# Two attention blocks with their gradients: order of the dV and dK stores, K of the first heads, and when the second block's x and g are transposed

## The chip, the core and the metric

The kernel runs on one core of a Trainium2 chip. The metric is the device time of one execution in microseconds. Five runs of the kernel before gave a median of 1718.41 us (1716.88 to 1725.21). The engines of the core are TensorE (PE in the profile, PEld for its weight loads), VectorE (DVE), ScalarE (ACT), GpSimd (POOL) and SyncE (SP). SP computes nothing here: it issues DMAs. POOL computes and issues DMAs.

## The reference

Two independent attention blocks, A and B, have the same shapes: x is 8 x 96 x 640 (batch, queries, model width), the caches of K and V are 8 x 32 x 512 x 128 (batch, heads, keys, head width), wq is 640 x 4096 and wo 4096 x 640, all bfloat16. The forward pass and then all gradients are wanted, for a given gradient of the joined output:

```python
q = (x @ wq).reshape(B, Sq, H, Dh).transpose(0, 2, 1, 3)
scores = jnp.einsum("bhqd,bhkd->bhqk", q, k_cache) * (Dh ** -0.5)
p = softmax(scores)
o = jnp.einsum("bhqk,bhkd->bhqd", p, v_cache)
out = o.transpose(0, 2, 1, 3).reshape(B, Sq, H * Dh) @ wo
```

The outputs are the joined output of both blocks, and for each block dx, dK, dV, dwq and dwo: eleven arrays. The caches read and the gradients dK and dV written are the bulk of the bytes.

## The kernel before

**Items and ticks.** The kernel is unrolled whole. Each piece of work is a Python closure that is handed to an `Emitter` with a tick and a slot; `run` sorts by tick, slot and order of adding, and calls the closures, which record instructions. One tick is one batch of one head: block A begins at tick 13, a head takes 8 ticks, block B begins 256 ticks later. Within a block, `c0t` is the first tick of a head, and `ct` that of a batch. `OFF` (L45) says how many ticks after `ct` each stage of a batch stands, and `HK` (L46) does so for the work of a whole head:

```python
OFF = dict(ldk=-5, ldv=-3, kt=-3, vt=0, s2=3, s3=3, s4=4, s5=5, s6=6, s7=7, s8=8)
HK = dict(pA=-10, pA2=-9, pB=-3, pC0=[-2, 0], pC1=[-1, 0], pD1=1, pD0=2, qA0=18, qA1=17, ...)
```

So eight or so batches are in flight in a tick, each in another stage. A scheduler then takes the recorded instructions and chooses the order on each engine and all waits, by its own estimate of durations, and may move an instruction away from where it was recorded. What goes through `tc.keep_in_program_order` (`pinned`, L111) stays in the recorded order relative to the others of its engine that are pinned. On POOL these are P_sb (L329), prod (L407), and the loads of wq and wo (L190, L199). The stores of dV and dK (L398) are not among them. On SP only the loads of `setup_ld` (L118) are pinned.

**One batch.** `c_ld` (L266) loads K and V of two batches at a time from SP, 256 KB each. `c_xt` (L275) transposes two batches by a DMA transpose from SP: all V (tile VT), and K of every second pair of batches (tile KT). `k_on_pe` (L548) chooses: for the other pairs `c_s1` (L280) transposes K on PE, four 128 x 128 transposes into kT_ps (L285) for each batch, copied out by DVE as KT_pe (L287). Then:

- S = Q K^T on PE (L298); DVE takes the negative row maximum negm (L300); ACT makes E = exp(S) and its row sums (L310).
- DVE inverts the sums (rinv, L320); POOL scales E to P_sb (L329), one tick before it is used.
- PE transposes P (L365); ACT evacuates (L378); PE forms O (L359), and dV from P and the natural dO (L389); ACT evacuates dV into dV_sb (L392).
- POOL multiplies O by dO (prod, L407); PE sums it (dl_ps, L419) and forms dP with VT (L417); DVE combines both with P to dS_sb (L421).
- PE forms dK from dS and the natural Q (L432), ACT evacuates into dK_sb (L435). PE transposes dS (L346) and forms dQ (L340).

dV_sb and dK_sb hold two batches each and have three tiles each. When the second batch is in, `c_st` (L395) stores the 256 KB from POOL's queue (L398). It is recorded one tick after that batch's dV or dK, at slot 54.3, behind P_sb (53) and prod (54). All PSUM tiles share eight banks.

**One head.** `pA` and `pA2` load wq and wo from POOL's queue. `pB` (L210, L216) transposes them. `pC` (L243) forms Q (which = 0) from xT and dO (which = 1) from gT, each in two pieces of 512 and 256 tokens. `pD` (L258) transposes these into natural order: Qnat_h and dOnat_h, evacuated by DVE. qA, qB, qD form dwo and dwq of finished heads, and `gU` (L512) the sums over groups of up to six heads for the output and for dx.

**x and g of a block.** `pC` needs x and g transposed: 12 tiles of 128 tokens, six of x and six of g. In block A they come from x_nat and g_nat. In block B `setup_ld` loads each tile from SP (160 KB) into one of five tiles named ld_tmp, and `setup_T` transposes it on PE (five transposes into tp_ps, L134) with a copy by DVE into xT or gT. The lines L162 to L171 set their ticks. The order is x 0 to 3, g 0 to 3, x 4 and 5, g 4 and 5. From the sixth on, a load must wait until the transposes of the tile five places earlier have read theirs.

Of the kernel before, what the change touches and what calls it, by code (L numbers as in the profile page):

```python
# [30 lines left out]
SL_LOAD = 0  # L31
# [9 lines left out]
SL_HEAD = 90  # L41
# [12 lines left out]
def build_block(tc, em, tick0, blk, x, kc, vc, wq, wo, g_all, out_all, dx, dk, dv, dwq, dwo, ident, ones, pools, HG=6, first=True, groups=None):  # L54
    nc = tc.nc
# [55 lines left out]
    def pinned(ins):  # L111
        return tc.keep_in_program_order(ins)

    def setup_ld(which_, t):
        def f():
            src_flat = x_flat if which_ == 0 else g_flat
            tmp = stp.tile([128, D], BF16, name="ld_tmp", tag="stage")
            pinned(nc.sync.dma_start(tmp[:], src_flat[t * 128:(t + 1) * 128, :]))  # L118
            S[("tmp", which_, t)] = tmp
        return f  # L120
# [41 lines left out]
                nc.vector.tensor_scalar(dst, src, float(sc), None, op0=ALU.mult)  # L162

    xg = [(0, t) for t in range(min(4, TT))] + [(1, t) for t in range(min(4, TT))] + [(w, t) for w in (0, 1) for t in range(4, TT)]
    xg_tick = [-8, -7, -6, -5, -4, -4, -3, -3, -2, -2, -1, -1]
    for i, (which_, t) in enumerate(xg):
        if first:
            em.add(tick0 + (-8 if which_ == 0 else 3), SL_SETUP, setup_T(which_, t))
        else:
            em.add(tick0 + (-12 if i < 5 else xg_tick[i - 5] - 1), SL_LOAD + (0 if i < 5 else 2), setup_ld(which_, t))  # L170
            em.add(tick0 + xg_tick[i], SL_SETUP, setup_T(which_, t))  # L171
    if first:
        for which_, tk in ((0, -12), (1, -11)):
# [53 lines left out]
    def pC(h, which, si):  # L227
        def f():
            st = HS[(blk, h)]
            (t0, w) = tsplits[si]  # L230
            if which == 0:
                dst = st["QT_h"]
                lhs = lambda c: st["wq_h"][:, c, :]
                rhsT = S["xT"]
                sc = scale
            else:
                dst = st["dOT_h"]
                lhs = lambda c: st["woT_h"][:, c * 128:(c + 1) * 128]
                rhsT = S["gT"]
                sc = None  # L240
            q_ps = bank([128, w], F32, "q_ps")
            for c in range(DC):
                nc.tensor.matmul(q_ps[:], lhs(c), rhsT[:, c, t0:t0 + w], start=(c == 0), stop=(c == DC - 1))  # L243
            evac(EV["pC%d%d" % (which, si)], dst[:, t0:t0 + w], q_ps[:], sc)
        return f
# [149 lines left out]
    def c_st(h, b, which):  # L395
        def f():
            dst = dv if which == "v" else dk
            nc.gpsimd.dma_start(dst[b - 1:b + 1, h].rearrange("b (p c) d -> p b (c d)", c=KC), SB.pop((blk, h, b // 2, which))[:])  # L398
        return f

    def c_s5b(h, b):
# [144 lines left out]
    NTS = len(tsplits)  # L546

    def k_on_pe(h, b):  # L548
        return (b // NB) % 2 == 0

    SX = pools["SX"]
    for g in range(NG):
        h0 = GH0[g]
        for hh in range(groups[g]):
            h = h0 + hh
            c0t = tick0 + h * B
            if not (first and h == 0):
                em.add(c0t + HK["pA"], 54.6, pA(h))
                em.add(c0t + HK["pA2"], 54.6, pA2(h))
            em.add(c0t + HK["pB"], SL_HEAD, pB(h))  # L560
            fh = first and h == 0
            for si in range(NTS):
                em.add(c0t + HK["pC0"][min(si, len(HK["pC0"]) - 1)], SL_HEAD, pC(h, 0, si))
                em.add(c0t + (3 if fh else HK["pC1"][min(si, len(HK["pC1"]) - 1)]), SL_HEAD + (7 if fh else 0), pC(h, 1, si))
            em.add(c0t + (3 if fh else HK["pD1"]), SL_HEAD + (8 if fh else 0), pD(h, 1))
            em.add(c0t + (4 if fh else HK["pD0"]), SL_HEAD, pD(h, 0))
            for b in range(B):
                ct = c0t + b
                if b % NB == 0:
                    em.add(tick0 - 12 if first and h == 0 and b == 0 else ct + OFF["ldk"], SLOTS["LOAD"], c_ld(h, b, "K", 7))  # L570
                    em.add(ct + OFF["ldv"], SLOTS["LOAD"], c_ld(h, b, "V", 5))
                    if not k_on_pe(h, b):
                        em.add(ct + OFF["kt"], SLOTS["LOAD"] + 1, c_xt(h, b, "KT", 2))
                    em.add(ct + OFF["vt"], SLOTS["LOAD"] + 1, c_xt(h, b, "VT", 4))
                if k_on_pe(h, b):
                    em.add(ct + 2, SLOTS["S1"], c_s1(h, b))
                em.add(ct + OFF["s2"], SLOTS["S2A"], c_s2a(h, b))
                em.add(ct + OFF["s2"], SLOTS["S2B"], c_s2b(h, b))
                em.add(ct + OFF["s3"], SLOTS["S3A"], c_s3a(h, b))
                em.add(ct + OFF["s3"], SLOTS["S3B"], c_s3b(h, b))  # L580
                em.add(ct + OFF["s5"], SLOTS["S5B"], c_s5b(h, b))
                if b % 2 == 1:
                    em.add(ct + OFF["s4"] + 1, 54.3, c_st(h, b, "v"))
                    em.add(ct + OFF["s7"] + 1, 54.3, c_st(h, b, "k"))
                em.add(ct + OFF["s4"], SLOTS["S4"], c_s4(h, b))
                for i, o in enumerate(("s8", "s7", "s5", "s4")):
                    SX.setdefault(ct + OFF[o], [None] * 4)[i] = (blk, h, b)
                em.add(ct + OFF["s6"], SLOTS["S6"], c_s6(h, b))
                em.add(ct + OFF["s7"], SLOTS["S7"], c_s7(h, b))
            hk = HK if first or h < H - 1 else dict(HK, qA0=13, qB=[14, 15], qA1=16, qD=[(19, 0, 2), (19, 2, 4), (19, 4, 5)])  # L590
            em.add(c0t + hk["qA0"], SL_HEAD, qA(h, 0))
            for di in range(len(wsplits)):
                em.add(c0t + hk["qB"][di], SL_HEAD + 1, qB(h, di))
            em.add(c0t + hk["qA1"], SL_HEAD, qA(h, 1))
            for (k_, c_lo, c_hi) in hk["qD"]:
                if c_lo < DC and h % 2 == 1:
                    em.add(c0t + k_, SL_HEAD + 2, qD(h, c_lo, min(c_hi, DC)))
        cLg = tick0 + (h0 + groups[g] - 1) * B + B - 1
        gs0 = max(3, (GSPREAD0 * groups[g]) // HG)
        gs1 = max(3, (GSPREAD1 * groups[g]) // HG)  # L600
        if not first and g == NG - 2:
            gs0, gs1 = 9, 9
        if g == 0:
            em.add(cLg + OFF["s5"] - 2, SL_LOAD, setup_acc)
        subs = [(0, t, gi) for t in range(TT) for gi in range(len(gsplits))] + [(1, t, gi) for t in range(TT) for gi in range(len(gsplits))]
        n_out = TT * len(gsplits)
        for i, (which, t, gi) in enumerate(subs):
            if which == 0:
                tk = cLg + OFF["s5"] + 2 + (i * gs0) // n_out
            else:  # L610
                tk = cLg + OFF["s8"] + 2 + gs0 - 3 + ((i - n_out) * gs1) // n_out
            em.add(tk, SL_GRP, gU(g, which, t, gi))
# [124 lines left out]
```

## Time and profile before

| | |
|---|---|
| median of 5 runs | 1718.41 us (1716.88 to 1725.21) |
| the profiled execution, its own time | 1712.33 us |
| its span, first to last instruction | 1710.5 us |
| PE busy | 1680.1 us, 98% |
| ACT, DVE, POOL busy | 81%, 77%, 61% |
| packets of SP's DMA queue, as a share of 16 engines | 73.1% |
| packets of POOL's DMA queue | 31.7% |
| mean granted TensorE clock | 0.996 |
| DMA issues: dV_sb, dK_sb stores | 256 each, 256 KB, 4.9 and 5.2 us to landing |
| DMA transposes VT, KT | 256 and 128, 6.0 and 4.9 us to landing |

A line of the profile names the source line, the engine, the operation, what it writes and reads, then the shapes and the count, busy time and mean duration. Behind the last bar is the time that the engine stood idle just before such instructions, and what ended that. Matmuls are pipelined, so the duration of one is longer than the distance between two starts. In lines of windows each engine's busy time is followed by its number of instructions; then come the granted clock, the share of the DMA engines and GB/s. In the list of waits a line reads: who waited, for what, total us, times, longest.

### The profile page before, as it was taken

To read this page: it belongs to the slowest core of one execution; us is meant where nothing else is said; L and a number is where in the kernel's file an instruction comes from. 1 tells how busy PE (TensorE), PEld (TensorE's weight loads), DVE (VectorE), ACT (ScalarE), POOL (GpSimd) and SP (SyncE) were. 2 spreads that over 40 slices of the span, in tenths; PEclk is the share of its full clock that TensorE was granted. 3 is DMA by queue.
4 is the path that set the end of the run, shared out by engine and by line. 5 is a ranking of instruction groups with operands and counts; after the bars stand their busy time and mean duration, and the time that the engine had idled before them with its cause. 6 is when DMAs were issued, how large, how long until landed. Compare 5 with 4: busy or idle time off the path is not lost.

```text
span 1710.5 us, 57281 instructions
## 1 busy us (share of the span) xinstructions
PE 1680.1 (98%) x21976; PEld 1343.5 (79%) x21976; DVE 1322.1 (77%) x3040; ACT 1384.7 (81%) x3518; POOL 1046.8 (61%) x1747
## 2 busy tenths in 40 slices
PE   8999999999999999999999999999999999999999
PEld 6787788778778778778778777887788778778876
DVE  6886678778788778788778776787788778778777
ACT  7998789768869869869768897997799679868974
POOL 4666566556657647657567564675576557656754
PEclk9999999999999999999999999999999999999999
DMA  9999999999999989999999999999999989999993
GB/s 267 255 269 267 244 227 244 259 241 255 255 223 267 265 219 272 270 208 282 263 254 248 250 274 247 251 240 257 245 255 275 236 221 262 252 239 244 263 236 132
DMA packets 606770, 424.66 MB, mean 248 GB/s; under 512 B 425696, under 2 KB 564320, under 8 KB 606496
## 3 DMA queue, kind: packets, MB, share of 16 engines
q1 hardware_dynamic: 552912, 243.65, 73.1%
q0 software_dynamic: 53584, 177.35, 31.7%
q8 instruction: 172, 2.82, 0.7%
q14 instruction: 102, 0.84, 0.2%
HBM read 161.09 MB, written 159.12 MB: 187 GB/s over the span
## 4 chain that ended last, share of the span: by engine, by line
PE 87%; DMA 5%; ACT 2%; POOL 2%; issue 2%; DVE 1%; SPq 0%; DVEq 0%; POOLq 0%; ACTq 0%
PE o_ps L512 12%; PE q_ps L243 11%; PE S_ps L298 6%; PE dK_ps L432 6%; PE dV_ps L389 6%; PE dwq_ps L490 6%; PE dP_ps L417 6%; PE dwo_ps L470 6%; PE x_ps L365 5%; PE x_ps L340 5%; PE dst_ps L346 5%; PE x_ps L359 4%; PE kT_ps L285 3%; PE n_ps L258 3%; DMA KT<-K_sb 3%; PE nat_ps L455 3%
## 5 line engine op out<-in xcount | busy, mean ns | idle before, releaser
L329 POOL TENSOR_SCALAR P_sb<-E_sb,rinv 96x512 bf16<-96x512 bf16 x512 | 352.2, 688 | 377.5 <-DVE rinv L320 367.8
L310 ACT ACTIVATE E_sb<-S_ps,negm 96x512 bf16<-96x512 f32 x512 | 355.2, 694 | 205.9 <-DVE negm L300 183.3
L421 DVE SCALAR_TENSOR_TENSOR dS_sb<-dP_ps,dl_ps,P_sb 96x512 bf16<-96x512 f32 x512 | 382.9, 748 | 68.9 <-PE dl_ps L419 51.0
L300 DVE TENSOR_REDUCE negm<-S_ps 96x1 f32<-96x512 f32 x512 | 347.5, 679 | 56.1 <-PE S_ps L298 52.9
L435 ACT ACTIVATE dK_sb<-dK_ps 128x512 bf16<-128x512 f32 x512 | 307.1, 600 | 65.8 <-PE dK_ps L432 61.2
L392 ACT ACTIVATE dV_sb<-dV_ps 128x512 bf16<-128x512 f32 x512 | 316.2, 618 | 0.0
L398 POOL DMA_DIRECT2D out_dram<-dV_sb x256 | 193.7, 757 | 135.2 <-ACT dV_sb L392 126.7
L378 ACT ACTIVATE PT_sb<-x_ps 128x384 bf16<-128x384 bf16 x512 | 257.7, 503 | 1.1 <-PE x_ps L365 1.1
L398 POOL DMA_DIRECT2D out_dram<-dK_sb x256 | 192.6, 752 | 84.0 <-ACT dK_sb L435 53.6
L512 PEld LDWEIGHTS <-OD 128*128 128x128 bf16 x1536 | 132.1, 98 | 99.8 <-issue 0.2
L417 PE MATMUL dP_ps<-VT,dOT_h 128*96 128x512 bf16 x512 | 195.7, 382 | 4.0 <-DMA VT<-V_sb 3.0
L389 PE MATMUL dV_ps<-dOnat_h,P_sb 96*128 96x128 bf16 x2048 | 198.4, 219 | 1.0 <-DVE dOnat_h L160 0.8
L432 PE MATMUL dK_ps<-Qnat_h,dS_sb 96*128 96x128 bf16 x2048 | 198.6, 220 | 0.0
L407 POOL TENSOR_TENSOR prod<-OD,dOT_h 128x96 bf16<-128x96 bf16 x512 | 186.1, 364 | 9.1 <-ACT OD L375 5.1
L348 DVE COPY dST_sb<-dst_ps 128x384 bf16<-128x384 bf16 x512 | 177.0, 346 | 11.8 <-PE dst_ps L346 10.8
L365 PE MATMUL x_ps<-ident,P_sb 96*128 96x96 bf16 x2048 | 172.5, 206 | 4.3 <-POOL P_sb L329 3.1
L375 ACT ACTIVATE OD<-x_ps 128x192 bf16<-128x192 f32 (+1 forms) x515 | 172.6, 335 | 4.5 <-PE x_ps L340 3.8
L320 DVE RECIPROCAL rinv<-rowsum 96x1 f32<-96x1 f32 x512 | 79.4, 155 | 124.0 <-ACT E_sb L310 118.1
L346 PE MATMUL dst_ps<-ident,dS_sb 96*128 96x96 bf16 x2048 | 172.6, 206 | 0.5 <-DVE dS_sb L421 0.5
L359 PE MATMUL x_ps<-PT_sb,V_sb 128*128 128x96 bf16 x2048 | 172.6, 206 | 0.4 <-ACT PT_sb L378 0.4
L340 PE MATMUL x_ps<-dST_sb,K_sb 128*128 128x96 bf16 x2048 | 171.2, 206 | 0.4 <-ACT PT_sb L378 0.4
L340 PEld LDWEIGHTS <-K_sb 128*128 128x128 bf16 x2048 | 132.0, 98 | 25.2 <-issue 1.0
(83 smaller groups left out, 3717.4 us busy)
## 6 DMA issues: line engine op xcount, KB each, us to landing
out_dram<-dV_sb POOLq DMA_DIRECT2D x256, 256.0 KB, 4.9
out_dram<-dK_sb POOLq DMA_DIRECT2D x256, 256.0 KB, 5.2
K_sb<-in_A_k_cache_dram SPq DMA_DIRECT2D x128, 256.0 KB, 5.1
V_sb<-in_A_v_cache_dram SPq DMA_DIRECT2D x128, 256.0 KB, 5.1
K_sb<-in_B_k_cache_dram SPq DMA_DIRECT2D x128, 256.0 KB, 4.9
V_sb<-in_B_v_cache_dram SPq DMA_DIRECT2D x128, 256.0 KB, 5.0
out_dram<-dwo_sb POOLq DMA_DIRECT2D x63, 160.0 KB, 4.9
out_dram<-dwq_sb POOLq DMA_DIRECT2D x31, 320.0 KB, 5.6
```

The costliest lines, as they stand in the source:

```text
L300: nc.vector.tensor_reduce(negm[:], S_ps[:], axis=AX.X, op=ALU.max, negate=True)
L310: nc.scalar.activation(E_sb[:], st["S_ps"][:], ACT.Exp, bias=st["negm"][:], scale=1.0, accum_out=rowsum[:])
L329: pinned(nc.gpsimd.tensor_scalar(P_sb[:], st["E_sb"][:], st["rinv"][:], 0.0, op0=ALU.mult, op1=ALU.add))
L340: nc.tensor.matmul(dQT_ps, st["K_sb"][:, c, :], st["dST_sb"][:, c * Sq:(c + 1) * Sq], start=(c == 0), stop=(c == KC - 1))
L389: nc.tensor.matmul(dV_ps[:, c * 128:(c + 1) * 128], P_sb[:, c * 128:(c + 1) * 128], hs["dOnat_h"][:, b * 128:(b + 1) * 128], start=True, s ...
L392: nc.scalar.activation(SB[(blk, h, b // 2, "v")][:, b % 2], dV_ps[:], ACT.Identity, scale=1.0)
L398: nc.gpsimd.dma_start(dst[b - 1:b + 1, h].rearrange("b (p c) d -> p b (c d)", c=KC), SB.pop((blk, h, b // 2, which))[:])
L417: nc.tensor.matmul(dP_ps[:], hs["dOT_h"][:, tok], st["VT"], start=True, stop=True)
L421: nc.vector.scalar_tensor_tensor(dS_sb[:], dP_ps[:], dl_ps[:, 0:1], st["P_sb"][:], op0=ALU.subtract, op1=ALU.mult)
L432: nc.tensor.matmul(dK_ps[:, c * 128:(c + 1) * 128], dS_sb[:, c * 128:(c + 1) * 128], hs["Qnat_h"][:, b * 128:(b + 1) * 128], start=True, s ...
L435: nc.scalar.activation(SB[(blk, h, b // 2, "k")][:, b % 2], dK_ps[:], ACT.Identity, scale=1.0)
L512: nc.tensor.matmul(o_ps[:], src[:, t * 128:(t + 1) * 128], rhs, start=(hh == 0), stop=(hh == groups[g] - 1))
```

## The change

It has three parts.

First, the store in `c_st` is pinned: stores of dV and dK now keep their recorded place on POOL among P_sb, prod and the pinned loads. In the built program the dV store stands one tick further back on POOL than before and the dK store one or two. Stores of dwo, dwq and of the output are still placed by the scheduler, around these.

Second, `k_on_pe` is also true for head 0 of each block. Batches 2, 3, 6 and 7 of these two heads get four PE transposes and a DVE copy each (8 groups, 32 transposes), and four DMA transposes of KT leave SP's queue.

Third, in block B the transposes of x and g stand two to three ticks later, from tick -6 to tick 2 around the block's start in place of -8 to -1. The first five loads are spread over ticks -11 to -7 in place of all standing at -12, and each later one is recorded one tick behind the transposes that free its tile, no longer one tick ahead of them. All stand behind the tick's loads and DMA transposes of K and V. To fit, head 0 of block B gets its own ticks for the second piece of Q (2), both pieces of dO (1 and 3), and both natural orders (3 and 4); those of dO are put behind the x and g transposes of the tick. Head 0 of block A keeps its ticks.

```diff
-    xg_tick = [-8, -7, -6, -5, -4, -4, -3, -3, -2, -2, -1, -1]
+    xg_tick = [-6, -5, -4, -3, -2, -2, -1, -1, 0, 1, 1, 2]
     for i, (which_, t) in enumerate(xg):
         if first:
             em.add(tick0 + (-8 if which_ == 0 else 3), SL_SETUP, setup_T(which_, t))
         else:
-            em.add(tick0 + (-12 if i < 5 else xg_tick[i - 5] - 1), SL_LOAD + (0 if i < 5 else 2), setup_ld(which_, t))
+            em.add(tick0 + (i - 11 if i < 5 else xg_tick[i - 5] + 1), SL_LOAD + 2, setup_ld(which_, t))
             em.add(tick0 + xg_tick[i], SL_SETUP, setup_T(which_, t))
...
-            nc.gpsimd.dma_start(dst[b - 1:b + 1, h].rearrange("b (p c) d -> p b (c d)", c=KC), SB.pop((blk, h, b // 2, which))[:])
+            pinned(nc.gpsimd.dma_start(dst[b - 1:b + 1, h].rearrange("b (p c) d -> p b (c d)", c=KC), SB.pop((blk, h, b // 2, which))[:]))
...
     def k_on_pe(h, b):
-        return (b // NB) % 2 == 0
+        return (b // NB) % 2 == 0 or h == 0
...
+            p0, p1, d1, d0, late = HK["pC0"], HK["pC1"], HK["pD1"], HK["pD0"], 0
+            if fh:
+                p1, d1, d0, late = [3, 3], 3, 4, 7
+            elif h == 0:
+                p0, p1, d1, d0, late = [-2, 2], [1, 3], 3, 4, 7
             for si in range(NTS):
-                em.add(c0t + HK["pC0"][min(si, len(HK["pC0"]) - 1)], SL_HEAD, pC(h, 0, si))
-                em.add(c0t + (3 if fh else HK["pC1"][min(si, len(HK["pC1"]) - 1)]), SL_HEAD + (7 if fh else 0), pC(h, 1, si))
-            em.add(c0t + (3 if fh else HK["pD1"]), SL_HEAD + (8 if fh else 0), pD(h, 1))
-            em.add(c0t + (4 if fh else HK["pD0"]), SL_HEAD, pD(h, 0))
+                em.add(c0t + p0[min(si, 1)], SL_HEAD, pC(h, 0, si))
+                em.add(c0t + p1[min(si, 1)], SL_HEAD + late, pC(h, 1, si))
+            em.add(c0t + d1, SL_HEAD + (8 if late else 0), pD(h, 1))
+            em.add(c0t + d0, SL_HEAD, pD(h, 0))
```

## The prediction

> **What bounds the kernel now.** I first read the page's busy times, then the wait list, then PE's groups, then the places where PE stands still.
>
> ```profile
> span 1710.5 us, 57281 instructions
> PE 1680.1 (98%) x21976; PEld 1343.5 (79%) x21976; DVE 1322.1 (77%) x3040; ACT 1384.7 (81%) x3518; POOL 1046.8 (61%) x1747
> ```
>
> PE is busy for 98% and so the bound. It leaves 1710.5 - 1680.1 = 30.4 us, and only a part of that is in reach: 5.4 us of gaps lie in the first 39 us and some 4 us behind the last matmul, both untouched. A change can win by closing gaps, and loses whatever it adds to PE. The next view is PE by group; the idle time before each group, with its releaser, is at the end of the line.
>
> ```profile
> L417 PE MATMUL dP_ps<-VT,dOT_h 128*96 128x512 bf16 x512 | 195.7, 382 | 4.0 <-DMA VT<-V_sb 3.0 <-DVE dST_sb L348 0.8 <-DVE rinv L320 0.2
> L365 PE MATMUL x_ps<-ident,P_sb 96*128 96x96 bf16 x2048 | 172.5, 206 | 4.3 <-POOL P_sb L329 3.1
> L298 PE MATMUL S_ps<-KT,QT_h 128*96 128x512 bf16 x256 | 98.0, 383 | 6.7 <-DMA KT<-K_sb 6.5
> L134 PE MATMUL tp_ps<-ident,ld_tmp 128*128 128x128 bf16 x60 | 6.5, 223 | 3.1 <-DMA ld_tmp<-in_grad_out_dram 2.9
> ```
>
> Three kinds of gap remain: transposed K or V late from the DMA queue (10.7 us), P late from POOL (4.3), and one wait for a loaded tile of g (3.1). The third is a single hole. PE's order of time and the granted clock (the column after the bracketed counts of POOL) around it:
>
> ```profile
> 830.24 0.44 PE L134 MATMUL tp_ps<-ident,ld_tmp 128*128 128x128 bf16 x5
> 833.62 0.23 PE L134 MATMUL tp_ps<-ident,ld_tmp 128*128 128x128 bf16 x1 [2.94 <-DMA ld_tmp<-in_grad_out_dram]
> ```
> ```profile
> 822.00:830.00 8.00, 7.83 (x103) 6.05 (x102) 7.05 (x18) 6.52 (x17) 5.61 (x9) 1.00 1.17 326
> 830.00:838.00 8.00, 5.06 (x47) 4.10 (x46) 2.90 (x7) 3.74 (x10) 2.94 (x6) 0.79 1.12 271
> 950.00:960.00 10.00, 7.16 (x85) 5.37 (x83) 6.02 (x13) 5.71 (x15) 5.17 (x9) 0.84 1.11 266
> ```
>
> A gap is paid twice: behind it the clock is halved for a while. In 830 to 838 us the mean is 0.79, so 0.21 x 8 = 1.7 us more are lost. The hole around 955 us costs 0.16 x 10 = 1.6 us within that window too.
>
> **The change, part by part.** Work is laid out in ticks, one batch of one head each; 64 heads of 8 batches in 1710.5 us make 3.3 us per tick.
>
> *x and g of the second block.* All 12 loads, 60 transposes and 12 DVE copies stay; they move. The last load left SP late, as the chain of waits shows:
>
> ```profile
> 825.82 7.76 DMA ld_tmp<-in_grad_out_dram
> ```
>
> It was issued at 825.8, wanted at 830.7 and landed at 833.6. A load cannot go before the transposes that free its tile (5 tiles), and here these stood at tick -3, the use at tick -1: two ticks of cover, less the SP queue. Now release and use are at ticks -1 and 2: three ticks, some 10 us against the 7.8 this load took. On SP the five first loads no longer go out in one burst ahead of loads of K and V, but one per tick behind them, and those that had to wait for a tile no longer stand ahead of K, V and VT. I take the whole hole as gone: -2.9 - 1.7 = -4.6 us. Bounds: 0 (another load is late instead) and -4.6.
> [...]
>
> *The other half of that move.* The first head's Q and dO products and their transposes (L243, L258) fall into ticks -2 to 4, with the transposes of dO straight behind their last product. In the first block, which always had this order, PE waited 0.7 us for gT and 0.8 us for dOnat_h. DVE must take four late xT/gT copies (0.49 each) and four more KT_pe copies (0.40) here, 3.6 us. In the rows of 838 to 862 us it is busy 7.43, 6.09 and 5.47 of 8 each, so 5.0 us are free, and the cover is thin. Cost between 0 and 2.5 us; I take 1.0, near the two waits of the first block. What would be late next is negm, then E and P of those ticks.
>
> *K of the first heads.* Batches 2, 3, 6, 7 of two heads: 8 groups of four transposes more, and 4 DMA transposes fewer (of 384). The pace of such a group stands in the chain:
>
> ```profile
> 433.54 0.22 PE kT_ps L285 x4
> ```
>
> 8 x 0.22 = +1.8 us on the bound engine, fully paid. [...] The 219 ns mean of such a matmul here is its own duration and overlaps the next; starts are 55 ns apart, and the clock stays at 1.00. I take 1.8; the end for the range is 8.8. The 8 evacuations (0.40 each) are DVE's, counted above for the second block; in the first DVE is busy 27.1 of 36 us from 10 to 46 us, so they fit. What it saves: S_ps waits for no KT in either first head (first wait at 70.9 us, in head 2), and SP issues 4 x 1.3 us less, with the DMA engines relieved by as many transfers. Direct gain 0. Whether the relief reaches the late KT of heads 2 to 5 is open: the SP queue is tied to PE by its 7 K tiles, so I take 0, and keep the bound below.
>
> *dV and dK stores.* In the built program they now stand behind P_sb and prod of their tick; before, the scheduler pulled the dV store one tick and the dK store one or two ticks ahead, where it waited for ACT:
>
> ```profile
> POOL out_dram L398 <- ACT dV_sb L392: 129.7, 236, 1.9
> POOL out_dram L398 <- ACT dK_sb L435: 55.4, 45, 3.2
> ```
>
> While the store waits, the next P_sb is queued behind it, and PE's transposes of P (L365) behind that. The sharpest case in POOL's order of time:
>
> ```profile
> 1580.30 0.76 POOL L398 DMA_DIRECT2D out_dram<-dV_sb  x1 [0.54 <-ACT dV_sb L392]
> 1582.98 0.72 POOL L398 DMA_DIRECT2D out_dram<-dK_sb  x1 [1.93 <-ACT dV_sb L392]
> 1583.75 0.70 POOL L329 TENSOR_SCALAR P_sb<-E_sb,rinv 96x512 bf16<-96x512 bf16 x1
> ```
>
> PE then stood 1.2 us. Moved back one tick, a store finds its data ready: no store waits for ACT in the new program. What is it worth? Three gaps before L365 (0.9, 0.6, 1.2) make 2.7. But matmul ends are modelled and hide small delays, so I went over starts: the first transpose of P normally starts 0.17 us after the matmul before it, and what exceeds that sums to 10.8 us; the part where P_sb began right behind a store of dK or dwq or a load of wq is 3.5 + 0.3 + 0.9 = 4.7 us. I take -4.5; bounds -2.7 and -10.8. The cost: the staging tiles (3 each) come free later. From issue and landing times, the dV store moves by 3.2 us and the dK store by 3.7 (medians); 3 of 506 would then land after their tile's next write, by 1.1, 0.1 and 0.7 us. ACT has 19% idle, so 0; if it had none, +1.8.
>
> *Sum:* -4.6 + 1.0 + 1.8 - 4.5 = -6.3 us. Against the profiled execution: 1712.33 us (span 1710.5 and 1.8 around it) goes to 1706.0. The median of the runs, 1718.4, lies 6.1 above that execution; I let that stand and take the same 6.3 off: 1712.1 us, 0.37% less. A difference of 0.3%, 5.2 us, is about what a measurement of this kernel tells from no change.
>
> **Rivals.**
> Nothing to measure: the g load is late again at tick 2 (0 in place of -4.6), the rest as above: 1.0 + 1.8 - 4.5 = -1.7, 1716.7 us. For it: three of the g and x loads took over 4.8 us around the hole, and SP is throttled by the same K, V and VT issues. Against: a tick more of cover.
>
> More than forecast: stores that alternate, one per tick, in place of pairs within 1.5 us shorten the transfers of KT and VT. These waits are 10.7 us of gaps, and two of the three clock dips (1.7 us at 134 and 3.4 us at 957) follow them. Half of 15.8 is 7.9: -14.2, 1704.2 us. For it: the lost 6.1 us between profile and median may be more such waits. Against: the packets of the two queues already fill 73.1 + 31.7% of the engines, and the bytes stay.
>
> Slower: the later stores run into their staging tiles. ACT's next dV or dK copy waits for the landing, then the bank of dV_ps or dK_ps, then PE. The place is the lean heads (2 to 5 of a block), where stores took 8 to 10.7 us. At the median landing of 4.9 and 5.2 us three are late. Were all stores 3 us slower, 16 of dV and 24 of dK would be, by 22.5 + 26.1 = 48.6 us together; a quarter passed on to PE is 12.2, and -6.3 + 12.2 = +5.9, 1724.3 us. It decides from a median landing of about 8 us on. Against: the bytes of the stores don't grow.
>
> **How the numbers follow.** Forecast 0.45 (two thirds of its width, about 1709 to 1716 us, below 1713.3, so 0.32 faster and 0.13 same); nothing 0.13; more 0.23; slower 0.19 (0.17 past +0.3%, 0.02 same). Faster 0.55, same 0.28, slower 0.17. Time: 1712.1. The range reaches to the second rival's 1704.2 less 1.2, as the POOL bound of -10.8 allows, and up to 1722, short of the last one's centre, with its upper part, the 8.8 us of transposes among it, left out: 1703 to 1722.
>
> **What would show it.** No wait of tp_ps for ld_tmp and clock 1.00 through that stretch; POOL's waits for dV_sb and dK_sb near zero, that time now standing as P_sb for rinv, and L365's idle below 2 us; 1056 kT_ps matmuls at 0.22 us per four, PE's busy time up by no more than 2 us; KT 124 times. Wrong if a tp_ps or n_ps group shows a new gap over 1 us, if ACT's dV_sb or dK_sb wait for an out_dram landing, or if L298 and L417 wait more than 10.7 us together.

## The result, and the profile after

The changed kernel takes 1713.0 us (median, 1696.9 to 1739.2) against 1718.2 us of the kernel before beside it (1705.5 to 1743.4): a ratio of 0.9959 with a 95% interval of 0.9942 to 0.9976, 0.41% less. The ratio leaves out slow runs, those over 1.5% above the fastest of their own kernel, which here cuts the changed kernel at 1722.4 us and the one before at 1731.1 us and so flatters the change: the means of all runs give 0.9971. The forecast was 1712.1 us. The same kernel was measured twice more, and gave 0.9986 and 1.0016 (below). So the number was met in the first comparison, but a gain of that size does not repeat, and the parts of the sum came out very differently from what I wrote.

The profiled execution of the changed kernel took 1719.92 us, 7 us above the median of its runs, while that of the kernel before lay 6 us below its own. The two pages must be read for their gaps, not for their spans.

The page's head and the groups by line of the changed kernel, the same ones as shown of the kernel before:

```profile
span 1718.1 us, 56912 instructions
PE 1685.4 (98%) x22008; PEld 1348.4 (78%) x22008; DVE 1324.3 (77%) x3048; ACT 1382.3 (80%) x3518; POOL 1037.6 (60%) x1747
```
```profile
L417 PE MATMUL dP_ps<-VT,dOT_h 128*96 128x512 bf16 x512 | 196.6, 384 | 5.5 <-DMA VT<-V_sb 5.5
L365 PE MATMUL x_ps<-ident,P_sb 96*128 96x96 bf16 x2048 | 172.4, 206 | 1.2 <-POOL P_sb L329 0.8
L298 PE MATMUL S_ps<-KT,QT_h 128*96 128x512 bf16 x248 | 94.2, 380 | 1.2 <-DMA KT<-K_sb 0.6 <-ACT dK_sb L435 0.5
L134 PE MATMUL tp_ps<-ident,ld_tmp 128*128 128x128 bf16 x60 | 6.9, 236 | 9.8 <-DMA ld_tmp<-in_grad_out_dram 8.0 <-DMA ld_tmp<-in_B_x_dram 1.7
```

Read the idle time behind the last bar. The wait for P (L365) fell from 4.3 to 1.2 us. The waits for KT and VT together fell from 10.7 to 6.7 us. The wait for x and g (L134), which was to vanish, rose from 3.1 to 9.8 us. In POOL's list of waits (who waited for what: total us, times, longest) the stores are gone from the top:

```profile
POOL P_sb L329 <- DVE rinv L320: 585.2, 423, 12.8
POOL out_dram L398 <- issue: 12.8, 12, 1.4
...
POOL out_dram L398 <- ACT dK_sb L435: 2.4, 1, 2.4
```

By group, POOL stood idle for 219.2 us before the stores of dV and dK in the kernel before (135.2 and 84.0); now it is 21.0 us (11.8 and 9.2). The time went to P_sb, which waited 367.8 us for rinv before and 585.2 now: POOL is no less idle, but it now stands at P_sb itself, for what P_sb needs.

The hole at the start of the second block, in PE's order of time:

```profile
834.09 0.44 PE L134 MATMUL tp_ps<-ident,ld_tmp 128*128 128x128 bf16 x5
842.57 0.29 PE L134 MATMUL tp_ps<-ident,ld_tmp 128*128 128x128 bf16 x1 [8.04 <-DMA ld_tmp<-in_grad_out_dram]
```

and in the windows of 8 us (busy time of PE, PEld, DVE, ACT, POOL with their counts, then the granted clock, DMA share, GB/s):

```profile
822.00:830.00 8.00, 8.00 (x111) 6.87 (x109) 6.09 (x15) 6.37 (x19) 4.02 (x7) 1.00 1.19 239
830.00:838.00 8.00, 4.24 (x52) 2.95 (x49) 4.06 (x10) 4.36 (x11) 4.40 (x8) 0.95 1.15 281
838.00:846.00 8.00, 3.44 (x34) 3.16 (x35) 1.84 (x5) 1.50 (x4) 0.66 (x1) 0.50 1.14 278
```

PE stood 8.04 us, from 834.53 to 842.57. The clock was 0.50 in the whole window from 838 us, which holds the rest of that gap and 3.4 us behind it. Why the tile of g came late is seen in the order of issue on SP's queue (start, time on the queue):

```profile
825.30 0.72 SPq L266 DMA_DIRECT2D K_sb<-in_A_k_cache_dram  x1
826.08 0.63 SPq L118 DMA_DIRECT2D ld_tmp<-in_grad_out_dram  x1
826.80 2.81 SPq L275 DMA_TRANSPOSE VT<-V_sb  x1
832.38 1.30 SPq L275 DMA_TRANSPOSE KT<-K_sb  x1
833.78 0.67 SPq L266 DMA_DIRECT2D V_sb<-in_A_v_cache_dram  x1
834.54 0.43 SPq L118 DMA_DIRECT2D ld_tmp<-in_grad_out_dram  x1
```

The tile that this last load writes was free at 821.1 us, when the transposes that read it had ended. The load left at 834.5, behind a VT transpose that held the queue for 2.8 us and a KT transpose that waited until its K, issued at 825.3, had landed at 832.3. It landed at 842.5.

### The profile page after: what moved, and what is told of

It reads as the page before. It is cut to its first block, busy times and chain, and to the rows that moved or that the text cites. A ratio compares the mean times of both kernels' runs of the same rounds, so it can differ in the third digit from the quotient of the medians.

```text
span 1718.1 us, 56912 instructions
## 1 busy us (share of the span) xinstructions
PE 1685.4 (98%) x22008; PEld 1348.4 (78%) x22008; DVE 1324.3 (77%) x3048; ACT 1382.3 (80%) x3518; POOL 1037.6 (60%) x1747
## 3 DMA queue, kind: packets, MB, share of 16 engines
q0 software_dynamic: 53584, 177.35, 32.7%
## 4 chain that ended last, share of the span: by engine, by line
PE 89%; DMA 6%; ACT 2%; issue 1%; DVE 1%; POOL 0%; SPq 0%; DVEq 0%; ACTq 0%; POOLq 0%
PE o_ps L512 12%; PE q_ps L243 12%; PE S_ps L298 6%; PE dP_ps L417 6%; PE dV_ps L389 6%; PE dK_ps L432 6%; PE dwo_ps L470 6%; PE dwq_ps L490 5%; PE x_ps L365 5%; PE x_ps L340 5%; PE dst_ps L346 5%; PE x_ps L359 5%; PE kT_ps L285 3%; PE n_ps L258 3%; PE nat_ps L455 3%; DMA VT<-V_sb 1%
## 5 line engine op out<-in xcount | busy, mean ns | idle before, releaser
L329 POOL TENSOR_SCALAR P_sb<-E_sb,rinv 96x512 bf16<-96x512 bf16 x512 | 350.6, 685 | 593.3 <-DVE rinv L320 585.2
L417 PE MATMUL dP_ps<-VT,dOT_h 128*96 128x512 bf16 x512 | 196.6, 384 | 5.5 <-DMA VT<-V_sb 5.5
L398 POOL DMA_DIRECT2D out_dram<-dV_sb x256 | 194.5, 760 | 11.8 <-issue 8.3
L407 POOL TENSOR_TENSOR prod<-OD,dOT_h 128x96 bf16<-128x96 bf16 x512 | 183.2, 358 | 14.7 <-ACT OD L375 13.4
L365 PE MATMUL x_ps<-ident,P_sb 96*128 96x96 bf16 x2048 | 172.4, 206 | 1.2 <-POOL P_sb L329 0.8
L340 PE MATMUL x_ps<-dST_sb,K_sb 128*128 128x96 bf16 x2048 | 171.3, 206 | 0.4 <-ACT PT_sb L378 0.4
L340 PEld LDWEIGHTS <-K_sb 128*128 128x128 bf16 x2048 | 131.9, 98 | 24.9 <-issue 0.8
```

The costliest lines, as they stand in the source:

```text
L329: pinned(nc.gpsimd.tensor_scalar(P_sb[:], st["E_sb"][:], st["rinv"][:], 0.0, op0=ALU.mult, op1=ALU.add))
L340: nc.tensor.matmul(dQT_ps, st["K_sb"][:, c, :], st["dST_sb"][:, c * Sq:(c + 1) * Sq], start=(c == 0), stop=(c == KC - 1))
L398: pinned(nc.gpsimd.dma_start(dst[b - 1:b + 1, h].rearrange("b (p c) d -> p b (c d)", c=KC), SB.pop((blk, h, b // 2, which))[:]))
L417: nc.tensor.matmul(dP_ps[:], hs["dOT_h"][:, tok], st["VT"], start=True, stop=True)
```

## The experiments

Each ratio is to the kernel before, run beside it in the same comparison. The gaps of PE are one profiled execution each: P is the wait of L365; KT + VT those of L298 (for KT) and L417; x/g that of L134 for ld_tmp.

| kernel | median, us | ratio (95% interval) | P | KT + VT | x/g |
|---|---|---|---|---|---|
| before | 1718.2 to 1714.8 | 1 | 4.3 | 10.7 | 3.1 |
| whole change, first | 1713.0 | 0.9959 (0.9942 to 0.9976) | 1.2 | 6.7 | 9.8 |
| whole change, second | 1711.9 | 0.9986 (0.9963 to 1.0010) | 1.2 | 4.5 | 8.6 |
| whole change, third | 1719.2 | 1.0016 (0.9989 to 1.0044) | 1.2 | 6.3 | 4.5 |
| stores only | 1718.4 | 1.0025 (0.9999 to 1.0050) | 1.1 | 11.7 | 6.7 |
| K on PE only | 1711.9 | 1.0002 (0.9980 to 1.0024) | 4.7 | 11.4 | 6.7 |
| x/g move only | 1722.8 | 1.0033 (1.0003 to 1.0063) | 4.3 | 25.6 | 4.8 |
| without the stores | 1716.9 | 1.0011 (0.9983 to 1.0039) | 4.6 | 9.1 | 3.9 |
| without the x/g move | 1712.7 | 0.9984 (0.9959 to 1.0009) | 1.2 | 2.6 | 6.9 |
| the same again | 1716.4 | 1.0003 (0.9978 to 1.0028) | 1.2 | 7.1 | 8.2 |
| x/g loads earlier in the tick | 1715.4 | 1.0005 (0.9971 to 1.0039) | 1.3 | 3.4 | 4.5 |
| K loads 2 ticks earlier | 1763.4 | 1.0274 (1.0216 to 1.0333) | 1.2 | 32.7 | 11.7 |
| more K on PE, no x/g move | 1712.1 | 0.9988 (0.9966 to 1.0011) | 1.2 | 2.3 | 6.2 |
| the same, x/g with cover | 1708.9 | 0.9981 (0.9956 to 1.0006) | 1.2 | 9.9 | 4.3 |

**The whole change, again.** No edit.

> The changed kernel once more, for a second profile and as the measure for its parts. The first profiled execution lost 9.8 us before tp_ps (8.0 of them in one wait for a tile of g at 834 us) and 12 us of clock, and took 1719.9 us against a median of 1713.0. If SP's lag behind its recorded place is a matter of the single execution, this one shows another sum of waits for ld_tmp, anywhere from 0 to 10 us, and the time follows it. If the move of x and g itself makes the wait, it stands here again with 5 us or more. Ratio to the kernel before 0.996 in both cases.

> The changed kernel once more, beside the two below on the same chip. If the whole gains what its two first comparisons had between them, its ratio to the kernel before is 0.996 to 0.999; P waits of L365 near 1.2 us, store waits of POOL near 21 us, S_ps for KT and dP_ps for VT 4 to 7 us together, tp_ps for ld_tmp 7 to 10 us.

Measured 0.9986 and 1.0016. The three intervals of one and the same kernel, 0.9942 to 0.9976 and 0.9989 to 1.0044 among them, do not all overlap: from one comparison to the next the ratio shifts by more than the interval of one comparison says. The means of all runs, 0.9971, 0.9976 and 1.0002, each with some 0.0023 on both sides, lie closer together. The mean of the three ratios is 0.9987. So no difference of 0.2% between two lines of the table is shown by the times; what follows rests on gaps that repeat in every profile. The groups of the second profile (first fence) and the third:

```profile
L365 PE MATMUL x_ps<-ident,P_sb 96*128 96x96 bf16 x2048 | 172.3, 205 | 1.2 <-POOL P_sb L329 0.8
L134 PE MATMUL tp_ps<-ident,ld_tmp 128*128 128x128 bf16 x60 | 6.9, 235 | 8.6 <-DMA ld_tmp<-in_grad_out_dram 8.6
```
```profile
L298 PE MATMUL S_ps<-KT,QT_h 128*96 128x512 bf16 x248 | 94.4, 380 | 6.3 <-DMA KT<-K_sb 5.7 <-ACT dK_sb L435 0.5
L134 PE MATMUL tp_ps<-ident,ld_tmp 128*128 128x128 bf16 x60 | 6.6, 227 | 4.5 <-DMA ld_tmp<-in_grad_out_dram 4.5
```

The gap for x and g is there in both, though in the third it is 4.5 us where I expected 7 to 10, and the third ratio missed its expectation of 0.996 to 0.999. KT is late in the third by as much as in the kernel before (6.3 and 6.7 us).

**The stores alone.** The kernel before with one edit:

```diff
-            nc.gpsimd.dma_start(dst[b - 1:b + 1, h]...)
+            pinned(nc.gpsimd.dma_start(dst[b - 1:b + 1, h]...))
```

> Only the pinned stores of dV and dK. By the prediction's step: POOL's waits for dV_sb and dK_sb fall from 185 us to below 20, the idle time of PE before its transposes of P from 4.3 to below 2 us, and the time by 4.5 us: ratio 0.9974. If the stores also shorten the transfers of KT and VT, PE's idle time before S_ps and dP_ps falls from 10.7 us to half and the ratio to 0.993. If later stores run into their three tiles, ACT waits for landings of out_dram and the ratio is above 1.

```profile
L417 PE MATMUL dP_ps<-VT,dOT_h 128*96 128x512 bf16 x512 | 196.4, 384 | 6.8 <-DMA VT<-V_sb 6.8
L365 PE MATMUL x_ps<-ident,P_sb 96*128 96x96 bf16 x2048 | 172.6, 206 | 1.1 <-POOL P_sb L329 0.6
L298 PE MATMUL S_ps<-KT,QT_h 128*96 128x512 bf16 x256 | 98.3, 384 | 4.9 <-DMA KT<-K_sb 4.9
```

The wait for P goes to 1.1 us, as in every kernel with pinned stores (1.1 to 1.3 us in all ten profiles), against 4.3 to 4.7 us in the four without. KT + VT stay at 11.7 us, as before (10.7): in this profile the stores alone don't shorten those waits. The ratio is 1.0025, and its interval (0.9999 to 1.0050) leaves out the 0.9974 that was expected. ACT waits for no landing of a store in this profile, so late stores are not seen to be the reason. The shorter wait for P is shown, a gain in time from the stores alone is not.

**K of the first heads alone.**

```diff
-        return (b // NB) % 2 == 0
+        return (b // NB) % 2 == 0 or h == 0
```

> Only K of the first heads on PE. By the prediction's step: 32 matmuls kT_ps more at 55 ns, PE's pace otherwise the same: +1.8 us, ratio 1.001. If four DMA transposes fewer relieve the lean heads behind the first ones, the late KT of heads 2 to 5 goes and the ratio is 0.998 or less.

```profile
L417 PE MATMUL dP_ps<-VT,dOT_h 128*96 128x512 bf16 x512 | 196.2, 383 | 10.7 <-DMA VT<-V_sb 10.7
L365 PE MATMUL x_ps<-ident,P_sb 96*128 96x96 bf16 x2048 | 172.5, 206 | 4.7 <-POOL P_sb L329 3.2
L298 PE MATMUL S_ps<-KT,QT_h 128*96 128x512 bf16 x248 | 94.5, 381 | 0.7 <-DMA KT<-K_sb 0.6
```

The wait for KT falls from 6.7 to 0.7 us and that for VT rises from 4.0 to 10.7: the sum stays (11.4). The time stays too, at 1.0002, although 1.8 us of PE work came in.

**The move of x and g alone.** The ticks, the loads and the ticks of head 0, without the other two parts; that is, the changed kernel with two lines taken back:

```diff
-            pinned(nc.gpsimd.dma_start(dst[b - 1:b + 1, h]...))
+            nc.gpsimd.dma_start(dst[b - 1:b + 1, h]...)
...
-        return (b // NB) % 2 == 0 or h == 0
+        return (b // NB) % 2 == 0
```

> Only the move of the second block's x and g, with the ticks of its first head. By the prediction's step: the wait for ld_tmp goes, with its half clock, and 1.0 us is lost behind the products of dO: -3.6 us, ratio 0.998. If the loads are late because they stand behind the loads and transposes of K and V on SP, which lags there, the waits for ld_tmp stay at 3 us or more and the ratio is between 0.999 and 1.002.

1.0033 (1.0003 to 1.0063), not faster and rather slower. PE still waits 4.8 us for a tile, here one of x at 833 us. Its profiled execution was a long one (span 1731.2 us), so its 25.6 us for KT and VT are not held against the move.

**Everything without the stores, and everything without the move.** The changed kernel with `pinned(...)` taken off the stores; and the changed kernel with the ticks, loads and head ticks of the kernel before (the lines of the head ticks are left out here):

```diff
-            pinned(nc.gpsimd.dma_start(dst[b - 1:b + 1, h]...))
+            nc.gpsimd.dma_start(dst[b - 1:b + 1, h]...)
```
```diff
-    xg_tick = [-6, -5, -4, -3, -2, -2, -1, -1, 0, 1, 1, 2]
+    xg_tick = [-8, -7, -6, -5, -4, -4, -3, -3, -2, -2, -1, -1]
...
-            em.add(tick0 + (i - 11 if i < 5 else xg_tick[i - 5] + 1), SL_LOAD + 2, setup_ld(which_, t))
+            em.add(tick0 + (-12 if i < 5 else xg_tick[i - 5] - 1), SL_LOAD + (0 if i < 5 else 2), setup_ld(which_, t))
```

> The change without its first part: K of the first heads on PE and the move of x and g. PE's idle time before its transposes of P is back at 4.3 us. If the stores bring 4.5 us, as the prediction has it, the ratio is above that of the whole change by 0.0026. If it is K on PE together with the move that shortens the waits for KT and VT (6.7 and 4.5 us in the two profiles of the whole, 10.7 before), these stay below 7 us here. If that needs the stores too, they are at 10 us or more.

> The change without its third part: pinned stores and K of the first heads on PE, x and g of the second block as before. In the two profiles of the whole change the waits for ld_tmp were 9.8 and 8.6 us with 5 us of half clock behind them, against 3.1 and 1.7 before. If the move makes them, they are 3 to 6 us here and the ratio is 0.995 or less. If they come with the pinned stores (alone: 6.7) or with K on PE (alone: 6.7), they stay at 6 us or more and the ratio is that of the whole change or above, 0.998 to 1.002.

> Stores and K on PE, without the move of x and g, once more, side by side with the whole. If the move of x and g brings nothing (theory), within 0.002 of the whole in this job. If it was worth the forecast 4.6 us less 1.0, it is 0.002 slower (rival); if the later x and g loads cost what their longer gap in the profile of the changed kernel shows (8.0 against 2.9 us), it is 0.003 faster.

Without the stores the ratio is 1.0011, and the wait for P is back at 4.6 us. That is 0.0024 above the mean of the whole change, near the 0.0026 that the stores were to bring, but its interval (0.9983 to 1.0039) is too wide to show it. KT + VT are 9.1 us there, between the two marks set for them. Without the move it is 0.9984 and, measured again, 1.0003, beside the whole change at 1.0016 in that same comparison. Taking the move out costs nothing that can be seen. The gap for x and g says the same: where x and g stand as in the kernel before, it is 3.1, 6.7, 6.7, 6.9, 8.2 and 6.2 us (mean 6.3); with the move it is 9.8, 8.6, 4.5, 4.8 and 3.9 us (mean 6.3). The 3.1 us of the kernel before, from which I forecast, are the lowest of the six with the old ticks.

**Loads of x and g ahead of the tick's other loads.** The changed kernel with its transposes spread from tick -8 to 2, the first five loads together at tick -14, and all loads ahead of those of K and V in their tick:

```diff
-    xg_tick = [-6, -5, -4, -3, -2, -2, -1, -1, 0, 1, 1, 2]
+    xg_tick = [-8, -7, -6, -5, -4, -3, -2, -1, 0, 1, 2, 2]
...
-            em.add(tick0 + (i - 11 if i < 5 else xg_tick[i - 5] + 1), SL_LOAD + 2, setup_ld(which_, t))
+            em.add(tick0 + (-14 if i < 5 else xg_tick[i - 5] + 1), SL_LOAD - 1, setup_ld(which_, t))
```

> The changed kernel with other ticks for x and g alone: the first five loads together at tick -14, each later one ahead of the tick's loads of K and V one tick behind the release of its tile, the transposes at -8, -7, -6, -5, -4, -3, -2, -1, 0, 1, 2, 2. That gives each load three to ten ticks until its use, in place of two to five. If the waits for ld_tmp are short cover against a lagging SP queue, they fall from 9 us to below 3, the half clock there goes, and the time falls by some 8 us against the whole change: ratio 0.992. If the loads are late whatever their place, since the DMA engines are full there, 6 us or more stay and the ratio is 0.997.

1.0005, with a gap of 4.3 us at 828 us; the 4.5 us in all lie between the two marks set for them (below 3, and 6 or more). The load behind that gap, the seventh, left SP 21.3 us after its tile was free, though it was recorded at the head of its tick. So a place ahead in the tick does not make it early.

**K loads two ticks earlier.** SP's transposes of K wait long for K to land. If that wait were what holds up SP, earlier K loads should help. The changed kernel with eight K tiles (to make room, the matmuls that warm up PE at the start are narrowed from 128 to 96 columns, not shown here):

```diff
-OFF = dict(ldk=-5, ldv=-3, ...)
+OFF = dict(ldk=-7, ldv=-3, ...)
...
-  c_ld(h, b, "K", 7))
+  c_ld(h, b, "K", 8))
```

> The changed kernel with eight tiles of K in place of seven, and the load of K two ticks earlier (the warm-up matmuls are narrowed to 96 columns to make room). SP's queue stands still when a KT transpose waits for its K to land (327 us in all before). If this wait is what makes KT, VT and the loads behind it late, PE's waits for them (KT, VT and ld_tmp: 14 to 16 us in the two profiles of the whole change) fall by half or more, and the ratio is 0.993 or less. If they are late because the DMA engines are full, nothing changes: 0.997.

It is 2.7% slower, which neither expectation had. The wait did go: in SP's list of waits the two lines that stood at 164.5 and 163.0 us in the kernel before are now

```profile
SPq L275 <- DMA K_sb<-in_B_k_cache_dram: 3.9, 2, 3.0
SPq L275 <- DMA K_sb<-in_A_k_cache_dram: 2.9, 1, 2.9
```

but the transfers became longer: medians from issue to landing went from 4.9 to 7.8 us for KT, 6.0 to 7.4 for VT, 5.1 to 6.5 (block A) and 4.9 to 5.8 (block B) for K, and 4.9 to 6.6 for the stores of dV. The times of the two queues' packets add up to 72.9 + 35.5% of the engines' time, beside 73.1 + 31.7% before; that more in flight only makes each wait longer is my reading of this, not shown apart. PE waits for VT and KT 32.7 us, for x and g 11.7:

```profile
L417 PE MATMUL dP_ps<-VT,dOT_h 128*96 128x512 bf16 x512 | 197.5, 386 | 18.4 <-DMA VT<-V_sb 18.3
L298 PE MATMUL S_ps<-KT,QT_h 128*96 128x512 bf16 x248 | 95.0, 383 | 14.3 <-DMA KT<-K_sb 14.1 <-ACT dK_sb L435 0.2
```

SP stood 327 us for K in the kernel before. Issuing K earlier took that wait away and won nothing back.

**More K on PE.** The version without the x/g move, with the K of three heads of each block on PE:

```diff
-        return (b // NB) % 2 == 0 or h == 0
+        return (b // NB) % 2 == 0 or h <= 2
```

> As the one above, but K of heads 0, 1 and 2 of each block is transposed on PE, not only of head 0: 16 more groups at 0.22 us, +3.5 us of PE, and 8 DMA transposes of KT fewer. If each group of heads moved to PE relieves the KT and VT transfers behind it as the first did (10.7 to some 4 us for two heads), the waits of S_ps and dP_ps fall by 2 to 4 us more, and it comes out even with the one above, within 0.001. If the relief was all in the first heads, PE's 3.5 us is paid in full: 0.002 slower.

KT + VT fell to 2.3 us, beside 7.1 and 2.6 of the two profiles of the version it starts from; 3.5 us of PE work came in; the ratio is 0.9988 beside 1.0003. It came out at least even, which speaks against "paid in full" (0.002 slower) and proves no gain.

**Real cover for x and g.** The version above with a sixth ld_tmp tile, transposes from tick -10 on, and loads three to five ticks ahead of their use:

```diff
-    xg_tick = [-8, -7, -6, -5, -4, -4, -3, -3, -2, -2, -1, -1]
+    xg_tick = [-10, -9, -8, -7, -6, -5, -4, -4, -3, -2, -2, -1]
...
-            em.add(tick0 + (-12 if i < 5 else xg_tick[i - 5] - 1), SL_LOAD + (0 if i < 5 else 2), setup_ld(which_, t))
+            em.add(tick0 + (i - 16 if i < 6 else xg_tick[i - 6] + 1), SL_LOAD, setup_ld(which_, t))
...
-            stp=P(name="stp", bufs=5),
+            stp=P(name="stp", bufs=6),
```

> As e11_more_pe (pinned stores, K of heads 0 to 2 on PE), but x and g of the second block get real cover on SP's queue: six tiles ld_tmp in place of five, the first six loads one per tick at ticks -16 to -11, transposes from tick -10 to -1, every later load recorded one tick behind the release of its tile and three to five ticks (10 to 16 us) ahead of its use, at the head of the tick on SP. In all profiles so far the loads 6 to 8 left SP 3.5 to 18 us behind the release of their tile and landed 2.7 to 9.5 us after. If the wait of tp_ps for ld_tmp is a matter of that cover alone (theory), it falls from 6.2 us to under 2, the clock keeps 1.00 around it, and the time is 0.001 to 0.004 below that of e11_more_pe (0.9988): 0.995 to 0.998. If the queue slips by as much again whatever is recorded (rival), tp_ps still waits over 4 us and the ratio stays at 0.998 to 1.001.

0.9981, and the wait is 4.3 us, over the bound of 4 that was set for it: the queue slips again. In SP's order of issue:

```profile
811.96 1.31 SPq L275 DMA_TRANSPOSE VT<-V_sb  x1
816.20 1.27 SPq L275 DMA_TRANSPOSE KT<-K_sb  x1
817.57 1.19 SPq L118 DMA_DIRECT2D ld_tmp<-in_B_x_dram  x1
```

The tile of this load, the tenth, was free at 802.3 us, when the transposes of the fourth had ended, but the load left at 817.6, at last behind a KT transpose that could not start until 816.2. It landed at 822.5 and PE, which had stood 2.0 us for it, took it at 822.6. Its median, 1708.9 us beside 1717.3, is the lowest measured, below the changed kernel's; the interval reaches 1.0006, so that it beats either kernel is not settled.

## Why the prediction was right and wrong

**The x and g step (-4.6 us) failed.** Its sentence was "three ticks, some 10 us against the 7.8 this load took". That is a sum for the last load alone, and for the last load it held: in the profile after it landed 2.7 us before its use. But the sixth to eighth came late instead. The sixth had more cover by the ticks, four from -6 to -2, and PE stood 8.04 us for it. The term left out was the time between the release of a tile and the issue of its next load. The times come from the starts and landings in the traces:

| kernel, load that PE waited for | tile released | load issued | landed | release to issue | issue to landing | both |
|---|---|---|---|---|---|---|
| before, 12th | 823.3 | 825.8 | 833.6 | 2.5 | 7.8 | 10.3 |
| whole change, 6th | 821.1 | 834.5 | 842.5 | 13.4 | 8.0 | 21.4 |
| whole change again, 7th | 812.0 | 819.1 | 827.6 | 7.1 | 8.5 | 15.6 |
| whole change, third, 8th | 815.2 | 821.2 | 828.2 | 6.0 | 7.0 | 13.0 |
| without the move, 6th | 798.1 | 812.9 | 816.5 | 14.8 | 3.6 | 18.4 |
| x/g with cover, 10th | 802.3 | 817.6 | 822.5 | 15.3 | 4.9 | 20.2 |

A reused tile needs 10 to 21 us, three to six ticks, between two uses in these six, and the larger part is often SP's queue: over all fourteen profiles, loads 6 to 8 left 1.4 to 21.3 us behind the release of their tile. I had written "two ticks of cover, less the SP queue" for the kernel before and then put nothing for the queue in the sum for the new one, though the change itself sets these loads behind the tick's K, V and DMA transposes, one of which stands waiting for K to land. My bounds were 0 and -4.6. What was measured in the three profiles of the whole change is +6.7, +5.5 and +1.4 us of gap against the one of before; between the means of the eleven profiles with the old or the new ticks it is 0 (6.3 and 6.3 us). The rival "nothing to measure" named this mechanism, a g load late again, though it expected it at tick 2. The sign of being wrong that I had set, a new gap of tp_ps over 1 us, did appear.

A smaller reading was off too. For the hole at 955 us I charged 0.16 x 10 = 1.6 us to the clock, but PE stood for 1.2 us of the half-clock time in that window, and such time costs no clock: 1.0 us is left. For the hole at 831 us the 1.7 us stand, since its half clock began behind the gap (833.99 us against 833.62).

**The dO step (+1.0) is not seen.** In the profile after, the groups of natural orders (n_ps) have at most 0.1 us of idle time, the products with gT 0.6 us, all in the first block, and no gap of PE in the second block's start belongs to them. DVE's extra copies were hidden. It is 0 as far as the profiles show, within its bounds.

**K on PE (+1.8) was right in price.** 1056 transposes of K are there, KT goes out 124 times, and these groups' busy time rose from 98.9 to 102.7 us for 32 more (3.8 us of durations, which overlap). From the first of four to the matmul behind them it is 0.22 us (median), as in the kernel before. PE's busy time rose by 5.3 us, not by the 2 us that I had allowed, but that profile has 24 us at half clock where the one of before has 14. In the second profile it rose by 1.9 us. The 8.8 us that I set as the upper end for this term, and named again in the range, no run shows: it would be a ratio 0.0041 higher than 1.8 us, while K on PE alone left the time at 1.0002, at most 1.0024, and the 0.22 us speak against it directly.

**What that part saves was mis-sized.** I took 0 for the relief of the KT and VT transfers and left it open. With pinned stores and K on PE together, these waits were 6.7, 4.5, 6.3, 2.6, 7.1 and 3.4 us in six profiles (mean 5.1, and 2.3 with three heads on PE); with one of the two alone or neither, 10.7, 11.7, 11.4 and 9.1, the long profile of the move left out. Two versions have both parts and more: the last, which loads x and g earlier, 9.9, and the one with K loads earlier, 32.7. So some 5 us of gap went here, which my rival "more than forecast" had put at half of 10.7. Its reason was the alternating stores alone, and the one profile with them alone, at 11.7, speaks against it. That it needs both rests on one profile for each part alone, and why it should, these runs don't show; a gap also moves by 4 us from execution to execution.

**The stores (-4.5) were right in place, not shown in time.** The gap for P went from 4.3 to 1.2 us in every profile of the whole change, 3.1 us, inside the bounds of -2.7 and -10.8. The wait moved to P_sb for rinv, as I had said it would. But the stores alone gave 1.0025, at best 0.9999. Whether the further 1.4 us that I added from starts are real, and how much of the 3.1 us reaches the time, can't be read from times that scatter by 0.2%.

**The slower rival is there, in small.** In the three profiles of the whole change ACT's dK_sb waited for the landing of a store 1.5, 2.6 and 0.8 us in all; in the one of before it never did. I had counted three late stores with 1.9 us together, so the size is right, and median landings of 5.2 and 5.4 us are far from the 8 us from which it decides. Still, such a wait was a sign of being wrong that I had set, and it does pass on to PE. In the second profile of the whole change ACT stood 1.88 us for a store before 789.85 us, and PE stood 1.88 us for ACT before its transposes of K at 790.5:

```profile
L285 PE MATMUL kT_ps<-ident,K_sb 128*128 128x128 bf16 x1056 | 102.3, 219 | 1.9 <-ACT dK_sb L435 1.9
```

In the kernel before, this group never waited (0.0 us). A longer case is in the version with the x/g loads ahead, in the order of ACT and of PE:

```profile
1477.00 0.60 ACT L435 ACTIVATE dK_sb<-dK_ps 128x512 bf16<-128x512 f32 x1 [2.65 <-DMA out_dram<-dK_sb]
```
```profile
1477.65 0.38 PE L285 MATMUL kT_ps<-ident,K_sb 128*128 128x128 bf16 x4 [2.65 <-ACT dK_sb L435]
```

The store landed late, ACT stood 2.65 us, its PSUM bank came free as much later, and PE stood 2.65 us for it; the clock in the 8 us after was 0.79. I had let a quarter of such a wait through to PE and taken ACT's slack to hide the three: these two passed whole.

**The sum.** I take the gaps of the whole change as the mean of its three profiles. KT and VT are 4.9 us less than in the profile of before, P 3.1 less. Before the transposes of K on PE (L285) and the S_ps that use them (KT_pe) there are 1.5 us more, part of them for late stores. The added work is 1.8. For x and g the profile of before is a poor base, since its 3.1 us are the lowest of six: with it the term is +4.5 us and the sum -0.2; with the mean of the six, 6.3, it is +1.3 and the sum -3.4. The clock adds little: half of the time that PE was busy at half clock is 8.6, 5.8 and 5.1 us in the three, 6.2 in the one of before.

The times go with the second sum. The mean ratio of the three comparisons, 0.9987, is 2.2 us less; the means of all runs are 5.1 and 4.2 us less and 0.3 more, 3.0 on average, give or take 2.3. So the likeliest size of the gain is 2 to 3 us, not 6.3. That the first comparison gave 5.2 us between the medians, close to the forecast, was luck: in part the scatter of comparisons, in part the relief of KT and VT, put at nothing, which stood in for the 4.6 us of x and g that did not come.

## What to carry to other kernels

Count the cover of a reused load tile from the release of the tile to the landing, with the wait of what stands ahead of the load in its queue (13.4 us from release to issue for the load that PE waited for in the profile after, 2.5 us in the one before); the recorded distance says little when a DMA transpose ahead of it waits for another transfer. Moving a DMA issue one step back, on a queue with compute behind it, takes its wait for data off that queue: here 219 us of POOL's waits before stores became 21 in the profile after, and PE's wait for P fell from 4.3 to 1.2 us. Whether that gains time is a second question, which the stores alone did not answer with yes. Before believing a few tenths of a per cent, measure the same kernel in several comparisons.

## What the runs showed of the hardware

**Behind some gaps of PE the granted clock was 0.50, for 3.41, 6.83 or 10.24 us; behind the shortest it was not.** Between the first 40 us and the last 7 us, the profiles of before and after have 17 gaps of PE longer than 0.7 us (by the profile's matmul ends, which are modelled). Eight of them were met or followed by half clock within 7 us, in six stretches:

| profile | gaps of PE: from, length (us) | clock 0.50: from, length (us) |
|---|---|---|
| before | 132.42, 1.95 | 134.26, 3.41 |
| before | 830.68, 2.94 | 833.99, 3.41 |
| before | 954.70, 1.44, and 956.67, 1.41 | 956.87, 6.83 |
| after | 123.50, 1.31, and 126.34, 1.79 | 127.17, 6.83 |
| after | 570.34, 2.90 | 574.31, 3.41 |
| after | 834.53, 8.04 | 837.14, 10.24 |

The other nine, of 0.71 to 1.42 us, were not. Two windows of the version "x/g with cover" differ in the same way: PE stood 1.74 us in the first, at clock 1.00, and 2.73 us in the second, at 0.79.

```profile
946.00:954.00 8.00, 6.26 (x98) 5.42 (x97) 6.56 (x16) 5.68 (x16) 4.42 (x9) 1.00 1.18 283
966.00:974.00 8.00, 5.27 (x49) 4.16 (x48) 2.73 (x7) 4.65 (x13) 3.30 (x7) 0.79 1.13 269
```

The length of one gap does not sort them: the two of 1.44 and 1.41 us, 0.53 us apart, went with half clock, the single one of 1.42 us at 818.99 us of the profile after did not. In each of the two profiles the changes of the granted clock lie whole multiples of one distance apart, 3.413 us, which fits them to 1 ns. Cut into pieces at that distance, the two hold 967 pieces at full clock between the first 40 us and the last 7 us: the six in which PE stood 1.64 to 2.94 us were followed by one at half clock, the 961 with at most 1.21 us were not. Of the ten pieces at half clock, the four with 0.96 to 3.41 us of standing were followed by another, the six with at most 0.11 us were not.

At clock 0.50 the starts of matmuls stood nearly twice as far apart: 107 ns against 56 for the transposes of K in the profile after, 80 against 42 for the products of dQ (L340) in both. So a gap that is followed by 3.41 us at half clock costs up to 1.7 us more (half of 3.41), an estimate from these numbers. That it pays to cut a gap shorter even where it can't be closed is my estimate as well: no run was made for it.

**With K issued earlier, the transfers took longer.** With K issued two ticks earlier and the same bytes, the median landings of KT, VT, K and the stores of dV rose by 0.9 to 2.9 us, and the kernel took 48 us more than the kernel before beside it.
